# First gate block's products by quarters during the attention, and maxima over partitions by one product in other banks

## The chip, the cores and the metric

The kernel runs on one core of a Trainium2 chip. Five engines work side by side: TensorE (PE, with its weight loads as PEld), VectorE (DVE), ScalarE (ACT), GpSimd (POOL) and SyncE (SP), which issues the DMAs. Each takes its own instructions in order. The metric is the time of one execution on the device in microseconds. Products are written to PSUM, in banks of 512 fp32 columns; tiles with the same tag take turns in a fixed number of buffers.

## The reference

Three parts follow each other:

```python
x = local_plus_pooled_attention(q, k, v)        # 2 batches, 8 heads, 576 positions, width 64
x = x.transpose(0, 2, 1, 3).reshape(1152, 512)
h = silu(x @ w_gate) * (x @ w_val)              # 512 -> 1536
x = h @ w_out                                   # 1536 -> 512
P = exp(x @ moe2_w_gate - max); eight rounds of row and column normalisation; P *= N / E
out = sum over e of P[:, e:e+1] * (relu(x @ w1[e]) @ w2[e])     # 8 experts, 512 -> 1024 -> 512
```

The attention is a softmax over positions nearer than 4, plus a softmax over q, k and v averaged by fours, its result repeated four times.

## The kernel before

**Attention.** `attention()` is a generator over eight pairs of heads (`pr` 0 to 7; pairs 0 to 3 are batch 0). For each pair `scores` forms the products in three banks, the minima on DVE and 26 exponentials on ACT; POOL scales; `turn` transposes on PE and copies to SBUF (L447 to L450); `combine` forms the result, and `split` (L168, L169) writes it as two fp16 parts into `xhl`. The scores run AHEAD = 2 pairs before the rest. These banks are the tag `att` of the pool `psa`, six of them. Two more banks, the tag `y` of the pool `psg`, hold everything else: warm products (products of zeros that nothing reads: NWARM at the start, NKEEP at each of three places of pairs 0 to 3), the sums of squares of v (`x1_scale`, once for each batch), the maxima over partitions (`allmax` with `short`), and the early gate products.

**Weights.** Gate and value weights come as 64-bit floats, in twelve blocks f of 128 + 128 columns. `load_gv` loads one, `conv_gv` rebuilds fp32 from its two words (ACT and four DVE operations), `prep_gv` takes its maximum over partitions, makes a power of two of it and splits into two fp16 parts. For the first NSHORT = 5 blocks and for x, the maximum is taken by PE: a product with the identity lays the 128 values in one row, DVE reduces it, and a second product with ones brings it back to all partitions. Later blocks use POOL.

**Gate products.** `gv_step(c, f, early)` forms the products of block f with the rows of chunk c: chunk 0 has 512 columns, chunk 1 two times 320. Each product of fp32 accuracy is three fp16 products for each of four k: 24 products of 512 columns for chunk 0 (gate and value). With `early` the result goes through the two banks `y`, a Tanh on ACT and three DVE operations (L561 to L564), since the attention's table of functions stays loaded; else through larger tiles that take the attention's banks when it has ended, a Silu (L574) and one DVE operation (L575). x of pair k is what `xhl[:, :, k]` holds, so the k loop runs over pairs.

**Order.** The program gives an order by hand: after pair `pr` the loop at the end of the attention issues `gv_step(0, EARLY.index(pr), True)` where `pr` is in EARLY, then `prep_gv` and `conv_gv` by PREP and CONV. A planner then lays the instructions out on each engine by priorities and its own costs, so their order on the engine is not that of the text, except where `issue_after` (in `gate`) or `keep_in_program_order` binds it. After the attention, chunk 1's block g and chunk 0's block g + 3 alternate, with weights prepared five blocks ahead; then come the product with w_out, the routing and the experts.

Of the kernel before, what the change touches and what calls it, by code (L numbers as in the profile page):

```python
# [42 lines left out]
NABS = 5  # L43
EARLY = (4, 6, 7)
AHEAD = 2
# [6 lines left out]
HB = 4  # L52
NWARM = 5
NKEEP = 2
NQ = 3
V4B = 4
NSHORT = 5
PREP = (1, 2, 3, 5, 7)
# [6 lines left out]
def tile_kernel(ctx, tc, qT, kT, vw, vd4, wgv, wo, wg2, w1, w2, out):  # L65
# [78 lines left out]
    def absmax(o, i, axis=AX.X):  # L144
        V.tensor_reduce(o, i, axis=axis, op=ALU.max, apply_absolute_value=True)  # L145

    def allmax(mx, n, nm, short=False):

        if n > 1:
            m = tmp(1, f"gm_{nm}")  # L150
            V.tensor_reduce(m, mx, axis=AX.X, op=ALU.max)  # L151
            mx = m
        if not short:
            g = tmp(1, f"g_{nm}")
            G.partition_all_reduce(g, mx, channels=P, reduce_op=RED.max)  # L155
            return g
        ps = psg.tile([P, 512], F32, tag="y", name=f"sm_{nm}")
        r = tmp(1, f"gr_{nm}")
        T.matmul(ps[:1, :P], lhsT=mx, rhs=ident, start=True, stop=True)
        V.tensor_reduce(r[:1], ps[:1, :P], axis=AX.X, op=ALU.max)  # L160
        T.matmul(ps[:, P:P + 1], lhsT=ones[:1], rhs=r[:1], start=True, stop=True)
        return ps[:, P:P + 1]

# [43 lines left out]
    gv_src = {}  # L207

    def gate(after):
        return tc.issue_after(after.ins) if after else nullcontext()  # L210

# [126 lines left out]
    def x1_scale(b):  # L338


        ps = psg.tile([P, 512], F32, tag="y", name=f"vv{b}")[:, :P]
        n = 0
# [21 lines left out]

    exped = {}

    def attention():
# [4 lines left out]
        qd, kd, exs, ats = {}, {}, {}, {}  # L372
        summed, scaled = {}, {}

# [59 lines left out]
        def turn(pr):  # L434
            ex = exs[pr]
            nm = f"{pr}"
            pt = bank(f"t{nm}", 3)
            at = ap.tile([P, DO + 4 * SD], F32, tag="at", bufs=2, name=f"at{nm}")
            for c in range(NW):
                i, o = divmod(c * P, 512)  # L440
                T.transpose(pt[i][:, o:o + P], ex[:, c * P:(c + 1) * P], ident)
            for c in range(2):
                for t in range(NQB):
                    o = (1 - c) * P + t * 2 * HQ
                    turned[0] = T.transpose(pt[1 + c][:HS, o:o + 2 * HQ],
                                            ex[:2 * HQ, DO + t * SD + c * HS:DO + t * SD + (c + 1) * HS], ident[:2 * HQ, :2 * HQ])
            A.copy(at[:, :512], pt[0])  # L447
            A.copy(at[:, 512:DO], pt[1][:, :P])
            A.copy(at[:HS, DO:DO + 2 * SD], pt[1][:HS, P:P + 2 * SD])
            A.copy(at[:HS, DO + 2 * SD:], pt[2][:HS, :2 * SD])  # L450
            ats[pr] = at
# [38 lines left out]
        def keep_warm(pr):  # L490
            for _ in range(NKEEP if pr < NPAIR else 0):
                ps = psg.tile([P, 512], F32, tag="y", name=f"kw{pr}")
                tc.keep_in_program_order(T.matmul(ps, lhsT=warm[:, :P], rhs=warm, start=True, stop=True))
# [38 lines left out]
    gv_done = {}  # L532

    def gv_step(c, f, early):
        o, nh = CH[c]
# [16 lines left out]
        if early:  # L552

            for u in range(nu):
                pp = []
                for t in range(2):
                    ps = psg.tile([P, 512], F32, tag="y", name=f"gv{c}_{f}_{t}{u}")[:, :n]
                    products(ps, t, u)
                    pp.append(ps)
# [123 lines left out]
    for pr in attention():  # L683
# [3 lines left out]
        if pr in EARLY:  # L687
            gv_step(0, EARLY.index(pr), True)
        if pr in PREP:
            prep_gv(PREP.index(pr), x1_done[pr])  # L690
        if pr == 0:
            conv_gv(0, exped[2])
# [186 lines left out]
```

## Time and profile before

| | us |
|---|---|
| median of 3 executions | 1023.69 |
| lowest, highest | 1023.57, 1026.44 |
| profiled execution, its time | 1024.88 |
| its span in the trace | 1023.1 |
| PE busy in the span | 1006.8 |
| DVE busy | 743.1 |
| ACT busy | 444.5 |

The span is the time between the first and the last instruction of the profiled execution. Busy is time in which an engine has an instruction in work. The granted clock is a share of 2.4 GHz. Ends of matmuls are modelled, so neighbouring products overlap in their rows and the distance of starts is the better measure. In a timeline row, "x12" counts merged instructions, and the bracket at its end gives the idle time before it and what ended it.

### The profile page before, as it was taken

The numbers are of one execution on the slowest core, as the hardware profiler recorded it, in microseconds if no ns is written. First come the engines' busy times: TensorE is split into PE (matmuls) and PEld (weight loads), VectorE is DVE, ScalarE is ACT, GpSimd is POOL, SyncE is SP. The second block draws the span as 40 slices with busy tenths as digits, with TensorE's granted clock in tenths as the row PEclk, the third lists the DMA queues.
The fourth block names the chain that finished last, engine by engine and source line by source line (L and its number), as shares of the span: only waits on it lengthen the run. The fifth ranks groups of instructions, "written<-read, shape, count | busy, mean of one in ns | idle before, by whom it ended". The sixth has DMA issues, their size and how long they took to land.

```text
span 1023.1 us, 16441 instructions
## 1 busy us (share of the span) xinstructions
PE 1006.8 (98%) x6639; PEld 634.3 (62%) x6641; DVE 743.1 (73%) x1516; ACT 444.5 (43%) x926; POOL 56.9 (6%) x78
## 2 busy tenths in 40 slices
PE   8989999999999999999999999999999999999998
PEld 7765566565668657566566655756665575565644
DVE  5888788865937998797497669849757873974721
ACT  7986566665425555253235125314413521541300
POOL 4541000000001100000000000000000000000000
PEclk9989999999989999999999999999999999999999
DMA  9922143320010212121003012110301211020011
GB/s 291 277 102 97 42 165 128 121 83 1 21 63 1 84 52 73 42 81 44 5 38 122 3 42 83 43 33 9 125 1 42 83 42 42 1 83 1 1 42 52
DMA packets 12988, 67.92 MB, mean 66 GB/s; under 512 B 1584, under 2 KB 1840, under 8 KB 6512
## 3 DMA queue, kind: packets, MB, share of 16 engines
q1 hardware_dynamic: 12912, 66.87, 18.9%
q8 instruction: 52, 0.85, 0.3%
q14 instruction: 24, 0.20, 0.1%
HBM read 64.50 MB, written 2.36 MB: 65 GB/s over the span
## 4 chain that ended last, share of the span: by engine, by line
PE 77%; DVE 11%; ACT 6%; DMA 4%; issue 1%; SPq 0%; POOL 0%; ACTq 0%; DVEq 0%
PE y L176 34%; PE p L176 28%; PE gv L176 7%; PE wo L176 4%; DVE w L169 2%; DMA r<-in_w 2%; ACT ex L417 1%; DMA rawo<-in_wo 1%; DVE mxw L145 1%; DMA q<-in_qT 1%; DVE h L748 1%; PE s L402 1%; PE lgps L603 1%; DMA rawg<-in_wgv 1%; DVE cvg L203 1%
## 5 line engine op out<-in xcount | busy, mean ns | idle before, releaser
L176 PE MATMUL y<-w,hhl 128*128 128x512 f16 (+1 forms) x1752 | 396.2, 376 | 0.0
L176 PE MATMUL p<-bop,w 128*128 128x320 f16 (+1 forms) x2688 | 354.4, 286 | 1.7 <-DVE h L748 1.0
L176 PEld LDWEIGHTS <-w 128*128 128x128 f16 x2688 | 263.0, 98 | 91.8 <-issue 2.5
L176 PEld LDWEIGHTS <-hhl 128*128 128x128 f16 x1752 | 171.4, 98 | 178.2
L776 ACT ACTIVATE hhl<-h 128x640 f16<-128x640 f32 (+1 forms) x128 | 82.7, 676 | 161.6 <-DVE h L748 161.6
L176 PE MATMUL gv<-xhl,gv 128*128 128x320 f16 (+1 forms) x864 | 144.1, 328 | 1.9 <-DVE mv L357 0.8
L168 ACT ACTIVATE w<-r,s_w 128x256 f16<-128x256 f32 (+1 forms) x96 | 71.1, 783 | 117.4 <-PE y L176 86.3
L176 PEld LDWEIGHTS <-gv 128*128 128x128 f16 x864 | 84.6, 98 | 59.0 <-issue 5.6
L807 DVE SCALAR_TENSOR_TENSOR acc<-y,pe,acc 128x512 f32<-128x512 f32 (+1 forms) x64 | 47.3, 739 | 101.3 <-PE y L176 100.5
L777 DVE SCALAR_TENSOR_TENSOR hhl<-h,hhl 128x640 f16<-128x640 f32 (+1 forms) x128 | 94.1, 754 | 17.5 <-ACT hhl L776 16.6
L748 DVE SCALAR_TENSOR_TENSOR h<-p,u 128x256 f32<-128x256 f32 (+1 forms) x192 | 84.7, 453 | 15.7 <-PE p L176 9.8
L169 DVE SCALAR_TENSOR_TENSOR w<-r,s_w,w 128x256 f16<-128x256 f32 (+1 forms) x96 | 78.2, 833 | 16.8 <-ACT w L168 16.7
L176 PE MATMUL wo<-ahl,wo 128*128 128x320 f16 (+1 forms) x432 | 73.9, 333 | 0.0
L168 ACT ACTIVATE w<-cmb,s_w 128x512 f16<-128x512 f32 x64 | 43.0, 710 | 42.1 <-DVE cmb L280 40.0
L176 PEld LDWEIGHTS <-wo 128*128 128x128 f16 x432 | 43.3, 101 | 28.2
L748 DVE SCALAR_TENSOR_TENSOR u<-p,u 128x320 f32<-128x320 f32 (+1 forms) x128 | 57.4, 449 | 3.6 <-PE p L176 3.2
L765 ACT ACTIVATE s<-p 128x256 f32<-128x256 f32 (+1 forms) x64 | 25.4, 397 | 55.7 <-PE p L176 55.5
L145 DVE TENSOR_REDUCE mxw<-r 128x1 f32<-128x1024 f32 x32 | 37.4, 1213 | 16.3 <-DMA r<-in_w 16.1
L169 DVE SCALAR_TENSOR_TENSOR w<-cmb,s_w,w 128x512 f16<-128x512 f32 x64 | 46.1, 742 | 0.1
L300 ACT ACTIVATE j<-r 128x1024 f16<-128x1024 f32 x32 | 33.4, 1046 | 26.6 <-DMA r<-in_w 26.6
L155 POOL PARTITION_ALL_REDUCE g_w<-gm_w x16 | 6.3, 394 | 595.1 <-DVE gm_w L151 589.2
L748 DVE SCALAR_TENSOR_TENSOR u<-p,s 128x256 f32<-128x256 f32 (+1 forms) x64 | 28.8, 451 | 5.1 <-PE p L176 4.3
(192 smaller groups left out, 824.8 us busy)
## 6 DMA issues: line engine op xcount, KB each, us to landing
r<-in_w SPq DMA_DIRECT2D x32, 1024.0 KB, 4.8
rawg<-in_wgv SPq DMA_DIRECT2D x12, 1024.0 KB, 5.1
rawo<-in_wo SPq DMA_DIRECT2D x6, 1024.0 KB, 5.9
q<-in_qT SPq DMA_DIRECT2D x8, 576.0 KB, 6.9
vz<-in_vw SPq DMA_DIRECT2D x8, 320.0 KB, 6.7
k<-in_kT SPq DMA_DIRECT2D x8, 288.0 KB, 6.8
v<-in_vd SPq DMA_DIRECT2D x8, 288.0 KB
out<-acc SPq DMA_DIRECT2D x8, 256.0 KB, 2.0
```

What stands on the lines that cost most here:

```text
L145: V.tensor_reduce(o, i, axis=axis, op=ALU.max, apply_absolute_value=True)
L168: return (A.activation(hi, src, AF.Copy, scale=s), V.scalar_tensor_tensor(lo, src, s, hi, op0=ALU.mult, op1=ALU.subtract))
L169: V.scalar_tensor_tensor(lo, src, s, hi, op0=ALU.mult, op1=ALU.subtract))
L176: T.matmul(ps, lhsT=wf(i, k), rhs=xf(j, k), start=n == 0, stop=n == 3 * nk - 1)
L203: V.scalar_tensor_tensor(o, hi, 0xC0000000, o, op0=ALU.bitwise_and, op1=ALU.bitwise_or)
L300: A.activation(junk, t[:, 2 * j:2 * j + 2].rearrange("p a n -> p (a n)"), AF.Abs, accum_out=mx[:, 2 * i + j:2 * i + j + 1])
L402: T.matmul(ps[i][:, c * WS:(c + 1) * WS], lhsT=q[:, ws].rearrange("p s j -> p (s j)"), rhs=k[:, ws], start=False, stop=c == NW - 1)
L748: V.scalar_tensor_tensor(o, ps, HSC, u, op0=ALU.mult, op1=ALU.add)
L765: A.activation(s1, p1, AF.Copy, scale=HSC)
L776: ra = A.activation(t[:, 0], h, AF.Relu)
L777: rv = V.scalar_tensor_tensor(t[:, 1], h, 0.0, t[:, 0], op0=ALU.max, op1=ALU.subtract)
L807: V.scalar_tensor_tensor(acc[t][:, ds], ps, p[:, t:t + 1], acc[t][:, ds], op0=ALU.mult, op1=ALU.add)
```

## The change

- The first gate block (c = 0, f = 0) is no longer issued at once after pair 4. The new `gv_part(k)` issues the six products of one k, into two banks `y` that are taken at the first call and held: k = 0 and 1 after pair 1, k = 2 after pair 2, k = 3 after pair 3. `gv_step(0, 0, True)` after pair 3 then only evacuates them.
- EARLY becomes (4, 6), for blocks 1 and 2. Before, block 0 came after pair 4, block 1 after 6, block 2 after 7.
- Warm products: nine instead of five at the start; at the pairs, for pairs 0 and 1 only (KEPT = 2).
- `allmax` with `short` uses one product, its stationary operand the column of maxima repeated 128 times, its moving operand the identity, so that each partition receives all 128 values; one DVE reduction follows. The result lies in SBUF. Its bank is one of the attention's six, and so is that of the sum of squares in `x1_scale`.
- The four copies of `turn` for pair 0 run on DVE instead of ACT.

`gate` and `scaled` only change their place in the text.

```diff
--- before.py
+++ after.py
@@ -41,7 +41,7 @@
 DW = NQB * SD
 DO = NW * P
 NABS = 5
-EARLY = (4, 6, 7)
+EARLY = (4, 6)
 AHEAD = 2
 NX = 3
 WB = 6
@@ -50,11 +50,12 @@
 UB = 8
 KB = 5
 HB = 4
-NWARM = 5
+NWARM = 9
 NKEEP = 2
+KEPT = 2
+NSHORT = 5
 NQ = 3
 V4B = 4
-NSHORT = 5
 PREP = (1, 2, 3, 5, 7)
 CONV = {1: (1, 2), 3: (3,), 5: (4,), 7: (5,)}
 NCONV = 6
@@ -144,22 +145,23 @@
     def absmax(o, i, axis=AX.X):
         V.tensor_reduce(o, i, axis=axis, op=ALU.max, apply_absolute_value=True)
 
+    def gate(after):
+        return tc.issue_after(after.ins) if after else nullcontext()
+
     def allmax(mx, n, nm, short=False):
 
         if n > 1:
             m = tmp(1, f"gm_{nm}")
             V.tensor_reduce(m, mx, axis=AX.X, op=ALU.max)
             mx = m
-        if not short:
-            g = tmp(1, f"g_{nm}")
+        g = tmp(1, f"g_{nm}")
+        if short:
+            ps = psa.tile([P, 512], F32, tag="att", bufs=6, name=f"sm_{nm}")[:, :P]
+            T.matmul(ps, lhsT=mx.to_broadcast([P, P]), rhs=ident, start=True, stop=True)
+            V.tensor_reduce(g, ps, axis=AX.X, op=ALU.max)
+        else:
             G.partition_all_reduce(g, mx, channels=P, reduce_op=RED.max)
-            return g
-        ps = psg.tile([P, 512], F32, tag="y", name=f"sm_{nm}")
-        r = tmp(1, f"gr_{nm}")
-        T.matmul(ps[:1, :P], lhsT=mx, rhs=ident, start=True, stop=True)
-        V.tensor_reduce(r[:1], ps[:1, :P], axis=AX.X, op=ALU.max)
-        T.matmul(ps[:, P:P + 1], lhsT=ones[:1], rhs=r[:1], start=True, stop=True)
-        return ps[:, P:P + 1]
+        return g
 
     def split(hi, lo, src, s, pool=False):
         if pool:
@@ -205,9 +207,6 @@
         return f
 
     gv_src = {}
-
-    def gate(after):
-        return tc.issue_after(after.ins) if after else nullcontext()
 
     gv_raw = {}
 
@@ -338,7 +337,7 @@
     def x1_scale(b):
 
 
-        ps = psg.tile([P, 512], F32, tag="y", name=f"vv{b}")[:, :P]
+        ps = psa.tile([P, 512], F32, tag="att", bufs=6, name=f"vv{b}")[:, :P]
         n = 0
         with gate(turned[0]):
             for i in range(NPAIR):
@@ -362,7 +361,7 @@
             o = slice(CH[1][0], S)
             split(xhl[:, 0, :, o], xhl[:, 1, :, o], tail, x1s[1][0])
 
-    exped = {}
+    exped, scaled = {}, {}
 
     def attention():
 
@@ -370,7 +369,7 @@
             return [psa.tile([P, 512], F32, tag="att", bufs=6, name=f"{nm}_{i}") for i in range(n)]
 
         qd, kd, exs, ats = {}, {}, {}, {}
-        summed, scaled = {}, {}
+        summed = {}
 
         def pooled(pr):
             q, k = ld[pr]
@@ -444,10 +443,11 @@
                     o = (1 - c) * P + t * 2 * HQ
                     turned[0] = T.transpose(pt[1 + c][:HS, o:o + 2 * HQ],
                                             ex[:2 * HQ, DO + t * SD + c * HS:DO + t * SD + (c + 1) * HS], ident[:2 * HQ, :2 * HQ])
-            A.copy(at[:, :512], pt[0])
-            A.copy(at[:, 512:DO], pt[1][:, :P])
-            A.copy(at[:HS, DO:DO + 2 * SD], pt[1][:HS, P:P + 2 * SD])
-            A.copy(at[:HS, DO + 2 * SD:], pt[2][:HS, :2 * SD])
+            copy = A.copy if pr else V.tensor_copy
+            copy(at[:, :512], pt[0])
+            copy(at[:, 512:DO], pt[1][:, :P])
+            copy(at[:HS, DO:DO + 2 * SD], pt[1][:HS, P:P + 2 * SD])
+            copy(at[:HS, DO + 2 * SD:], pt[2][:HS, :2 * SD])
             ats[pr] = at
 
         def combine(pr):
@@ -488,7 +488,7 @@
         NP = NPAIR * B
 
         def keep_warm(pr):
-            for _ in range(NKEEP if pr < NPAIR else 0):
+            for _ in range(NKEEP if pr < KEPT else 0):
                 ps = psg.tile([P, 512], F32, tag="y", name=f"kw{pr}")
                 tc.keep_in_program_order(T.matmul(ps, lhsT=warm[:, :P], rhs=warm, start=True, stop=True))
 
@@ -531,6 +531,17 @@
     amx = {}
     gv_done = {}
 
+    held = []
+
+    def gv_part(k):
+        n = 2 * CH[0][1]
+        if not held:
+            held.extend(psg.tile([P, 512], F32, tag="y", name=f"gv0_0_{t}0")[:, :n] for t in range(2))
+        for t in range(2):
+            for i, j in ((0, 0), (0, 1), (1, 0)):
+                T.matmul(held[t], lhsT=gv_w[0][:, i, (t * KD + k) * P:(t * KD + k + 1) * P], rhs=xhl[:, j, k, :n],
+                         start=k == 0 and j == i, stop=k == KD - 1 and i > 0)
+
     def gv_step(c, f, early):
         o, nh = CH[c]
         if f == 0:
@@ -553,7 +564,9 @@
 
             for u in range(nu):
                 pp = []
-                for t in range(2):
+                for t in range(0 if f else 2):
+                    pp.append(held[t])
+                for t in range(2 if f else 0):
                     ps = psg.tile([P, 512], F32, tag="y", name=f"gv{c}_{f}_{t}{u}")[:, :n]
                     products(ps, t, u)
                     pp.append(ps)
@@ -685,9 +698,14 @@
             load_gv(0)
             continue
         if pr in EARLY:
-            gv_step(0, EARLY.index(pr), True)
+            gv_step(0, 1 + EARLY.index(pr), True)
         if pr in PREP:
             prep_gv(PREP.index(pr), x1_done[pr])
+        if 0 < pr < KD:
+            for k in range(0 if pr == 1 else pr, pr + 1):
+                gv_part(k)
+            if pr == KD - 1:
+                gv_step(0, 0, True)
         if pr == 0:
             conv_gv(0, exped[2])
             load_gv(1)
```

## Rows read from the trace of the kernel before

**Rows 1.** Busy time, share of the span and instructions of each engine, whole execution.
```profile
PE 1006.8 (98%) x6639; PEld 634.3 (62%) x6641; DVE 743.1 (73%) x1516; ACT 444.5 (43%) x926; POOL 56.9 (6%) x78
```

**Rows 2.** Windows: length, busy us (instructions) of each engine, granted clock, DMA.
```profile
0.00:98.10 98.10, 89.39 (x859) 66.54 (x862) 75.97 (x173) 77.01 (x305) 38.81 (x46) 0.95 0.61 191
98.10:108.90 10.80, 10.80 (x53) 4.73 (x52) 8.24 (x13) 5.87 (x10) 0.00 (x0) 1.00 0.18 77
108.90:230.90 122.00, 120.90 (x772) 75.43 (x772) 96.53 (x180) 79.41 (x140) 4.38 (x8) 1.00 0.31 113
```

**Rows 3.** Windows of 10 us, same columns.
```profile
60.00:70.00 10.00, 7.23 (x91) 5.63 (x91) 8.08 (x15) 8.01 (x36) 6.69 (x8) 1.00 0.40 139
70.00:80.00 10.00, 9.22 (x53) 5.19 (x53) 8.51 (x25) 6.58 (x29) 3.37 (x4) 0.50 0.00 1
80.00:90.00 10.00, 10.00 (x104) 5.85 (x103) 8.46 (x18) 7.77 (x16) 2.17 (x3) 0.99 0.43 140
```

**Rows 4.** Timeline of PE: start, us, line, operation, count, idle before.
```profile
1.17 2.31 PE L90 MATMUL pw<-warm 128*128 128x512 bf16 x5 [1.17 <-DVE dist L93]
5.32 0.72 PE L399 MATMUL s<-maskb,identb 128*128 128x320 bf16 x2 [1.83 <-DVE identb L107]
5.82 4.51 PE L402 MATMUL s<-k,q 128*128 128x64 f32 x20
...
20.99 2.44 PE L402 MATMUL s<-k,q 128*128 128x64 f32 x20 [0.87 <-ACT k L380]
...
54.81 0.38 PE L493 MATMUL kw<-warm 128*128 128x512 bf16 x1
...
64.61 0.38 PE L159 MATMUL sm_v<-ident,mxv 128*1 128x128 f32 x2 [0.48 <-DVE mxv L354]
...
76.29 4.65 PE L176 MATMUL gv<-xhl,gv 128*128 128x512 f16 x12 [0.78 <-DVE mv L357]
...
82.92 2.75 PE L176 MATMUL gv<-xhl,gv 128*128 128x512 f16 x12
...
98.10 10.53 PE L176 MATMUL gv<-xhl,gv 128*128 128x512 f16 x48
...
199.47 31.42 PE L176 MATMUL gv<-xhl,gv 128*128 128x320 f16 x216 [0.46 <-ACT act L574]
```

**Rows 5.** Timeline of DVE in the attention.
```profile
22.36 0.49 DVE L409 TENSOR_REDUCE stm<-s 128x5 f32<-128x320 f32 x1
...
51.27 1.28 DVE L169 SCALAR_TENSOR_TENSOR gv<-cvg,s_gv,gv 128x1024 f16<-128x1024 f32 x1
...
62.74 1.21 DVE L169 SCALAR_TENSOR_TENSOR xhl<-x,s_x,xhl 128x512 f16<-128x512 f32 x1
...
70.63 0.27 DVE L160 TENSOR_REDUCE gr_v<-sm_v 1x1 f32<-1x128 f32 x1
...
76.09 0.15 DVE L357 TENSOR_SCALAR mv<-sm_v 128x1 uint32<-128x1 uint32 x1
```

**Rows 6.** Warm products of the pairs: ns minimum/median/maximum, first and last start.
```profile
L493 PE MATMUL kw<-warm x22: 376/379/390, 19.5 to 54.8; 128*128 128x512 bf16 x22
```

**Rows 7.** Timeline of DVE at the end of the attention.
```profile
98.90 0.81 DVE L481 TENSOR_TENSOR x<-o,avd 128x288 f32<-128x288 f32 x2
...
102.71 0.48 DVE L562 TENSOR_SCALAR act<-act,iv 128x512 f32<-128x512 f32 x1
...
105.44 0.74 DVE L564 SCALAR_TENSOR_TENSOR act<-gv,iv,act 128x512 f32<-128x512 f32 x1
```

**Rows 8.** Timeline of ACT in the attention.
```profile
19.75 0.61 ACT L447 COPY at<-t 128x512 f32<-128x512 f32 x1
...
79.59 0.51 ACT L168 ACTIVATE xhl<-tail,s_x 128x256 f16<-128x256 f32 x1 [2.73 <-DVE s_x L140]
```

**Rows 9.** Chain that ended last, pieces between 160 and 200 us.
```profile
166.92 0.71 ACT act L574
...
175.65 7.48 DMA rawo<-in_wo
```

## The prediction

> **What bounds the kernel now.** I read the page first. TensorE (PE) is busy 1006.8 of 1023.1 us [rows 1], so PE work sets the end, unless work is put where PE would have stood still or has run slowly. The windows come next, cut at the end of the attention [rows 2]. From 98.1 to 230.9 us, where the gate and value products run, PE is idle 1.1 us in all (10.80 - 10.80, 122.00 - 120.90). In the first 98.1 us it is idle 8.7 us, and its mean granted clock is 0.95. So a microsecond of products moved from behind 98.1 to a free place before it is worth about a microsecond.
>
> The finer windows show where the free places are [rows 3]: 60 to 70 us has 2.8 us of PE idle time. In 70 to 80 the granted clock is 0.50, the lower level, 1.2 GHz: the 9.22 us of work there would fit in some 4.6 us at 2.4 GHz. Before that fall PE was partly idle and had almost only fp32 products; it rose again while the first 16-bit gate products ran. The PE timeline prices this [rows 4]: the first half of the first gate block takes 4.65 us for twelve products, the second 2.75 us for the same twelve. In the attention DVE and ACT are nearly as full as PE (8.08 and 8.01 of 10 us in 60 to 70), so its length hangs on all three.
>
> **The block that moves.** Four blocks of 24 products with 512 columns lie between 76.29 and 108.6 us: three early ones and the main one for f = 3. The last 48 of these products run from 98.10 on, back to back, 10.53 / 48 = 0.219 us each [rows 4]. After the change block 0 comes behind pairs 1 to 3 and the other early blocks one slot earlier each, so of the 48 only 24 are left behind the attention. This takes 24 x 0.219 = 5.3 us off a stretch where PE is the bound.
>
> What does block 0 cost where it goes? Its weights are ready at 51.27 + 1.28 = 52.55 us and the last quarter of its input at 62.74 + 1.21 = 63.95 [rows 5], so it can be issued between about 52.6 and 65 us: 18 products first, 6 after. That is 5.3 us of PE time. Twelve of the 24 warm products go at the same time (KEPT is 2, so those of pairs 2 and 3), 0.22 us each if back to back as the gate products, 0.38 by their own rows [rows 4, 6]: -2.6 to -4.6 us. Net +0.7 to +2.7 us of PE work, against 2.8 us of idle time in 60 to 70 [rows 3]. I take the cost as nothing, covered by that idle time; uncovered it is +2.7 us.
>
> **Evacuation.** Block 2's three DVE operations come at 102.71 (0.48), 103.71 (0.68 by the pattern of the other two blocks) and 105.44 (0.74) [rows 7], behind the attention. They move into it: about 1.9 us on DVE, and two passes over the block on ACT, about as long. DVE has 1.5 us free in each of 70 to 80 and 80 to 90 [rows 3]. Hidden or not, bounds 0 and +1.9; I take +0.5.
>
> **The copies for pair 0.** Four copies leave ACT, where they start at 19.75 with one of 0.61 us [rows 8], in a part where ACT works through exponentials without a gap, and go to DVE. By the nearest row, a reduction of 320 columns from the same kind of bank in 0.49 us [rows 5], their 1216 columns cost about 1.9 us of DVE. DVE has room there; ACT can scale the next k 0.5 us sooner. Bounds -0.9 to +1.0; I take -0.4.
>
> **The maxima.** Before, a maximum is a product, a DVE reduction, a second product and a read by the next DVE operation. After, it is one product (with a 128-column instead of a 1-column weight) and one reduction. Each of seven maxima loses one pair of products, about 0.3 us of PE, and one round trip. One round trip was dear: the second batch's maximum is reduced at 70.63 and only read at 76.09 [rows 5], the first gate product waited 0.78 us for that read, and ACT stood still 2.73 us until the scale came [rows 4, 8]. The two rows do not add: ACT's idle time here is not all on the path. Bounds 0 to -2.7; I take -1.0.
>
> The banks are the new wait. Nine results (two sums of squares, seven maxima) now take turns with the scores in the attention's six banks, where each pair takes eight. The reduction of such a result sits in DVE's order; until it is done the sixth tile after it, a score or transpose group of a later pair, can't start, and behind that PE instruction everything queues. Before, such results sat in the other two banks and hurt little when late (the second batch's maximum was multiplied at 64.61 and reduced at 70.63 [rows 4, 5]). Nothing shows the cost in the new place: below 0 (the banks turn over faster), above several microseconds. The nearest row is the read at 76.09 that held the gate product for 0.78 us; I take +0.8, once.
>
> **The warm products.** Five take 2.31 us from 1.17 on, 0.43 us apart. Nine end near 5.2 us, and the first score product waits until 5.32 for the identity [rows 4]: they lie in the 1.83 us that PE waits anyway. The first scores show the lower clock, the third pair no longer (20 products in 4.51 us, at 20.99 in 2.44 [rows 4]). If the nine bring the rise forward, PE gains some 4 us in a part where ACT's chain of exponentials sets the pace, so I count 0, bounds 0 and -1.5.
>
> **The clock in 70 to 80.** With block 0 issued between 52 and 65 us in place of fp32 work and idle time, the fall is likelier to stay away than not. If it stays away, the twelve products that took 4.65 us take 2.75: -1.9 us on the path [rows 4]. I take -1.2, between 0 and -1.9; all of the lost 4.6 us is the lower end.
>
> **Hand-over.** Before, block 2 covers the time in which the attention's banks come free for the larger tiles of the main blocks (the last pair's sums on DVE run from 98.90, 0.81 us [rows 7]). After, that cover is gone or thinner: 0 to +1.6; I take +0.8.
>
> **Behind it.** Weights must keep up with a PE that is early. The chain from 166.92 to 199.47 runs over ACT, DVE and a load of 7.48 us [rows 9] and ends in PE, which had been idle only 0.46 us there [rows 4]. The chain starts from a PE result at 166.92, so it moves with PE in the main, but its DVE work does not get shorter. Bounds 0 and +5.3; I take +0.6.
>
> **Sum.** -5.3 + 0 + 0.5 - 0.4 - 1.0 + 0.8 + 0 - 1.2 + 0.8 + 0.6 = -5.2 us. The profiled execution took 1024.88 us (span 1023.1), 1.2 above the median 1023.69, which is what a change of this size is to be set against. 1023.7 - 5.2 = 1018.5 us.
>
> **Rivals.**
> - *Clock and attention close up (0.18).* The clock stays at 2.4 GHz from 5 us on, the 4.6 us of 70 to 80 and much of ACT's 2.73 us come back: -5.3 - 4.6 + 0.5 = about 1014. For it: ACT and DVE both wait on PE in 70 to 82. Against: DVE is 85% busy there.
> - *The clock falls where warm products go (0.06).* Pairs 2 and 3 lose twelve warm products, and before 52.6 us no quarter can stand in for them. A fall like that at 70, ten microseconds at 1.2 GHz, costs 4.6 us, and the gain of 1.2 in 70 to 80 is lost: 1023.7 - 5.2 + 1.2 + 4.6 = 1024.3, no change. For it: the fall at 70 came with no warm product since 54.81 [rows 4]. Against: the pairs' products leave PE hardly any idle time before 58 us. The Trainium skill, "TensorE: Matmul & The Clock Gate", Part 1, states this as a rule: the lower clock is the default, and activity releases it; here the trace agrees with it for 76 to 80 us, where dense gate products came before the rise, and not for the time from 5.3 us to the second pair, where PE was busy with fp32 scores almost without a gap and stayed at the lower clock.
> - *The block only changes place (0.16).* The attention is itself bound, 30 to 58 us by PE, then by DVE; block 0 pushes it back by its net 2.7 us and block 2's evacuation by 1.9, or the weights chain gives the 5.3 us back near 199 us. 1021 to 1024: no change. For it: DVE and ACT are above 80% in 60 to 70 us. Against: PE's idle time there.
> - *The bank ring stalls (0.10).* Slower. The place is a score group of pair 4 to 7 held by a maximum whose reduction is late in DVE's order. One of 5 us eats the gain; two of 7 us, somewhat longer than the 6.0 from 64.61 to 70.63, give 1023.7 - 5.2 + 14 - 3 = 1029.5, with 3 us of them in idle time. It decides from 5.2 + 3.1 = 8.3 us of lost attention time on. Against: the order on DVE is laid out anew with the banks known.
>
> **How the numbers follow.** The main case has 0.50, with its own range 1015 to 1020.6. A change under 0.3%, 3.1 us, can't be told from none. Faster: 0.50 + 0.18 = 0.68; same: 0.06 + 0.16 = 0.22; slower: 0.10. The range 1010.5 to 1024.5 takes in the bounds of the clock terms below and the unchanged case above, and leaves out the slow rival and a little below.
>
> **What would show it.** In the new profile: 24 gate products of 512 columns between 52 and 66 us; no more than about 24 between the last attention product and the first 320-column product; that first product near 103 instead of 108.9; a granted clock near 1.00 in 60 to 90 us; nothing over 1 us of PE waiting for a maximum's reduction. The prediction is wrong if the attention ends more than 3 us later than 98 us, or if PE is idle several microseconds between 110 and 231 us. A new fall of the clock behind 231 us, where the order of instructions is laid out anew as well, would move the time by some 3 us without any of these steps being wrong.

## The result, and the profile after

| | before | after |
|---|---|---|
| median of 4 executions, us | 1024.07 | 1033.66 |
| lowest, highest | 1023.57, 1026.44 | 1032.04, 1036.05 |
| profiled execution: span | 1023.1 | 1030.1 |
| first gate product behind the attention, start | 98.10 | 111.39 |
| first gate product of 320 columns, start | 108.88 | 119.15 |
| first product with w_out, start | 230.73 | 242.23 |
| first product of the experts' stage, start | 312.32 | 320.52 |

The ratio is 1.0100, 95% interval 1.0078 to 1.0122: slower by 1%, where 0.5% faster was forecast, and outside the range. By the starts in the table the attention takes 13.3 us more, the gate stage 1.8 less, the product with w_out 3.3 less and the rest 1.2 less, in all +7.0 us of span. At the first gate product of 320 columns both kernels have done the same work, the attention and 96 products of 512 columns; the new one comes there 10.3 us later.

The page's busy line of the kernel after answers to [rows 1]: PE is busy 6.6 us less, in a longer span.

```profile
PE 1000.2 (97%) x6618; PEld 631.8 (61%) x6619; DVE 745.7 (72%) x1520; ACT 444.2 (43%) x922; POOL 55.3 (5%) x78
```

The windows of the stages, cut at the start of the last attention products, at the first gate product behind them, at the first of 320 columns and at the first with w_out (columns as in [rows 2]), and then windows of 10 us, to be held against [rows 3]:

```profile
0.00:106.95 106.95, 88.28 (x847) 66.80 (x848) 79.50 (x181) 78.21 (x306) 37.07 (x46) 0.87 0.57 179
106.95:111.39 4.44, 1.33 (x23) 1.15 (x21) 2.52 (x6) 1.44 (x4) 0.00 (x0) 0.50 0.24 98
111.39:119.15 7.76, 7.76 (x24) 2.96 (x25) 6.49 (x16) 4.46 (x6) 0.35 (x1) 0.66 0.17 33
119.15:242.23 123.08, 120.48 (x770) 75.10 (x769) 93.73 (x167) 77.46 (x137) 4.23 (x7) 1.00 0.30 110
...
10.00:20.00 10.00, 4.99 (x32) 4.37 (x33) 4.44 (x13) 7.28 (x44) 6.34 (x9) 0.71 1.05 284
40.00:50.00 10.00, 9.13 (x71) 7.62 (x75) 9.21 (x20) 7.76 (x32) 4.09 (x5) 0.58 0.57 188
60.00:70.00 10.00, 5.39 (x96) 4.80 (x95) 6.50 (x19) 7.93 (x32) 2.63 (x3) 0.94 0.41 140
70.00:80.00 10.00, 10.00 (x48) 8.82 (x47) 8.12 (x26) 6.48 (x28) 1.58 (x3) 0.54 0.00 0
```

In the attention PE has about as much work as before (88.28 against 89.39 us) and twice the idle time (18.7 against 8.7), at a mean granted clock of 0.87 instead of 0.95. (Both means leave out the start: before, the column reads 1.00 in the first 20 us, while twenty scores take 4.51 us there and 2.44 at 20.99 [rows 4].) Three stretches hold time at the lower level, 1.2 GHz: 10 to 20, 40 to 50 and 70 to 80 us; before, from 20 us on, there was one, the 0.50 of [rows 3].

The PE timeline of the kernel after shows what comes ahead of each of them:

```profile
1.17 3.50 PE L91 MATMUL pw<-warm 128*128 128x512 bf16 x9 [1.17 <-DVE dist L94]
...
5.81 2.44 PE L401 MATMUL s<-k,q 128*128 128x64 f32 x20
...
16.97 1.33 PE L440 MATMUL t<-ident,ex 128*128 128x128 f32 x5 [4.79 <-POOL ex L427]
...
37.16 0.49 PE L160 MATMUL sm_gv<-ident,mxg 128*128 128x128 f32 x2 [1.33 <-ACT rawg L225]
37.48 0.60 PE L440 MATMUL t<-ident,ex 128*128 128x128 f32 x4
39.24 0.33 PE L440 MATMUL t<-ident,ex 128*128 128x128 f32 x1 [1.16 <-ACT ex L416]
...
40.29 0.44 PE L444 MATMUL t<-ident,ex 96*72 96x96 f32 x3 [0.47 <-ACT ex L420]
...
42.05 4.53 PE L401 MATMUL s<-k,q 128*128 128x64 f32 x20
...
50.45 3.41 PE L542 MATMUL gv<-xhl,gv 128*128 128x512 f16 x12
...
69.51 0.77 PE L160 MATMUL sm_v<-ident,mxv 128*128 128x128 f32 x2 [4.61 <-DVE mxv L353]
70.07 0.64 PE L160 MATMUL sm_gv<-ident,mxg 128*128 128x128 f32 x2
70.50 1.27 PE L440 MATMUL t<-ident,ex 128*128 128x128 f32 x5
...
77.11 1.06 PE L542 MATMUL gv<-xhl,gv 128*128 128x512 f16 x2
...
111.39 11.20 PE L178 MATMUL gv<-xhl,gv 128*128 128x512 f16 x48 [3.11 <-DVE g_gv L161]
123.14 3.15 PE L178 MATMUL gv<-xhl,gv 128*128 128x320 f16 x22 [0.56 <-DVE act L588]
```

(A merged row names only its first shape: of the 48 products at 111.39, 24 have 512 columns and 24 have 320.) At 37.16 and 69.51 PE stands at a maximum over partitions whose operand is not ready, and the transposes of the next pair (`t`) stand behind it, here those of pairs 2 and 4. The maxima of weight blocks (`sm_gv`) at 37.16 and 70.07, and two more at 53.70 and 94.11, each stand right ahead of a pair's transposes. Before, they had places of their own; its PE timeline for the same pairs:

```profile
35.94 0.77 PE L441 MATMUL t<-ident,ex 128*128 128x128 f32 x5
...
39.49 0.38 PE L159 MATMUL sm_gv<-ident,mxg 128*1 128x128 f32 x2
...
53.50 0.76 PE L441 MATMUL t<-ident,ex 128*128 128x128 f32 x5
```

Pair 2's transposes come 1.5 us later than before, and behind them the scores of pair 4 take 4.53 us, at half rate. The maximum is not the last thing that pair 2 waits for. Its own exponentials were scaled by 29.8 us, and yet its fifth transpose waits 1.16 us, and its last three 0.47, for exponentials of pair 3. That is the turn of the banks: a pair takes eight tiles (three for transposes, three for scores, two for results) out of six buffers, so before the change its three transpose tiles take over the buffers of the last transpose tile of the pair before and of the first two score tiles just written. With one maximum in between they take over those of all three score tiles, which ACT must have read first; and ACT ends these exponentials at 40.2 us, before at 36.6. Pair 4's transposes come at 70.50 instead of 53.50, and behind them the granted clock is 0.54. At 111.39 the main gate products wait 3.11 us for the reduction of a weight maximum, which frees the bank that they take: its product comes at 105.90, and DVE reduces it at 111.04, behind sums and splits of the last pair. The nine warm products do what was hoped of them at 5.81 (2.44 us in place of 4.51 [rows 4]), and then PE stands still for 4.79 us, because POOL, which waited 12.6 us for the load of v, can't scale pair 0 sooner, and the clock is lost again (0.71 in 10 to 20 us).

DVE of the same kernel between 62 and 71 us, where PE waits 4.61 us:

```profile
62.63 1.56 DVE L171 SCALAR_TENSOR_TENSOR gv<-cvg,s_gv,gv 128x1024 f16<-128x1024 f32 x1 [0.67 <-ACT gv L170]
64.11 0.59 DVE L410 TENSOR_REDUCE stm<-s 96x3 f32<-96x432 f32 x1
67.40 0.19 DVE L424 TENSOR_REDUCE rs<-sts 128x16 f32<-128x32 f32 x1 [2.69 <-ACT ex L420]
...
69.07 0.29 DVE L353 TENSOR_TENSOR mxv<-mxv,mxv 128x1 f32<-128x1 f32 x1
```

The value that PE waits for needs two short DVE operations. They stand behind a sum of pair 5 that waits 2.69 us for ACT's exponentials. So pair 4's transposes, whose exponentials were long done, wait on PE for those of pair 5.

### The profile page after: what moved, and what is told of

The parts are those of the page before. It is cut to its first block, busy times and chain, and to the rows that moved or that the text cites. A ratio compares the mean times of both kernels' runs of the same rounds, so it can differ in the third digit from the quotient of the medians.

```text
span 1030.1 us, 16399 instructions
## 1 busy us (share of the span) xinstructions
PE 1000.2 (97%) x6618; PEld 631.8 (61%) x6619; DVE 745.7 (72%) x1520; ACT 444.2 (43%) x922; POOL 55.3 (5%) x78
## 4 chain that ended last, share of the span: by engine, by line
PE 79%; DVE 11%; ACT 5%; DMA 2%; issue 2%; SPq 0%; POOL 0%; ACTq 0%; DVEq 0%; POOLq 0%
PE y L178 36%; PE p L178 31%; PE wo L178 4%; PE gv L178 4%; DMA rawo<-in_wo 1%; DVE cvg L205 1%; DVE cvg L206 1%; DMA v<-in_vd 1%; PE s L401 1%; ACT ex L416 1%; DVE cvg L200 1%; DVE act L588 1%; DVE w L171 1%; ACT rawg L225 1%; PE lgps L616 1%
## 5 line engine op out<-in xcount | busy, mean ns | idle before, releaser
L178 PE MATMUL gv<-xhl,gv 128*128 128x320 f16 (+1 forms) x840 | 139.4, 328 | 5.7 <-DVE g_gv L161 3.1
L178 PEld LDWEIGHTS <-gv 128*128 128x128 f16 x840 | 82.5, 99 | 61.0 <-issue 7.5
L178 PE MATMUL wo<-ahl,wo 128*128 128x320 f16 (+1 forms) x432 | 71.5, 326 | 0.0
L171 DVE SCALAR_TENSOR_TENSOR ahl<-act,sc,ahl 128x512 f16<-128x512 f32 (+1 forms) x24 | 19.6, 818 | 17.6 <-ACT ahl L170 17.6
```

The costliest lines, as they stand in the source:

```text
L171: V.scalar_tensor_tensor(lo, src, s, hi, op0=ALU.mult, op1=ALU.subtract))
L178: T.matmul(ps, lhsT=wf(i, k), rhs=xf(j, k), start=n == 0, stop=n == 3 * nk - 1)
```

## The experiments

Times are medians in us, ratios are to the kernel before on the same chip, with 95% intervals.

**Which part of the change costs it.** e1 puts only the new `allmax` and the new bank of `x1_scale` into the kernel before (both hunks as in the diff).

> The kernel before, with one part of the change alone: maxima by one product, and they and the sums of squares in the attention's six banks. Bank theory (the results in the attention's banks hold up the scores): the attention ends 5 us or more later, 1029 or slower. Quarter theory (the products of block 0 between the scores hold them up) and clock theory (missing warm products bring half-clock stretches): no part of either is in it, 1021 to 1025, the round trip saved being worth at most 2.7 us.

1035.70, ratio 1.0114 (1.0089 to 1.0140): the whole loss. e2 has only the nine warm products.

```diff
-NWARM = 5
+NWARM = 9
```

> The kernel before with nine warm products at the start and nothing else. All three theories: 1022 to 1025 (first scores at the full clock, but the third pair waits for a load of v through POOL, as in the changed kernel). A gain of 2 us or more would mean that the start sets the attention's length after all; a loss of 3 us or more would mean that the clock, raised early and lost again behind 12 us, is a cost of its own.

1024.81, 1.0018 (0.9987 to 1.0049): no change that can be told. e3 is the change without the quarters (EARLY as before); e4 is the change with NWARM = 5.

> The changed kernel without its quarters: block 0 whole behind pair 4 and blocks 1 and 2 behind 6 and 7 as before; maxima in the attention's banks, nine warm products at the start, none at pairs 2 and 3, copies of pair 0 on DVE. Quarter theory: the loss is gone, 1021 to 1025. Bank theory: most of it stays, 1029 to 1034. Clock theory: it stays or grows, as neither warm products nor quarters stand at pairs 2 and 3: 1031 to 1038.

> The changed kernel with five warm products at the start instead of nine. Bank and quarter theory: 1031 to 1036 as the changed kernel, since pairs 0 and 1 wait for a load anyway. Clock theory: within 3 us of it, the half-clock stretches at 40 to 50, 70 to 80 and 105 to 115 us being made by what comes later.

1034.58, 1.0103 (1.0066 to 1.0140), and 1036.69, 1.0129 (1.0100 to 1.0158). Neither the quarters nor the warm products at the start explain the loss.

**One product, or its bank?** e5 keeps the one product and leaves it in the old banks, the sums of squares too (shown against the line of e1):

```diff
-            ps = psa.tile([P, 512], F32, tag="att", bufs=6, name=f"sm_{nm}")[:, :P]
+            ps = psg.tile([P, 512], F32, tag="y", name=f"sm_{nm}")[:, :P]
```

> The kernel before with maxima by one product and one reduction, in the two banks they had before; the sums of squares stay there too. Bank theory: no loss, 1019 to 1025, with a gain of up to 2.7 us from the shorter round trip. Product theory (the 128-column product or the order it brings is itself the cost, whatever the bank): 1030 or slower.

1021.83, 0.9971 (0.9948 to 0.9994): a gain of 3 us. e6 is the kernel before, with its two products, and only the weights' maxima in the attention's banks:

```diff
-        ps = psg.tile([P, 512], F32, tag="y", name=f"sm_{nm}")
+        ps = (psa.tile([P, 512], F32, tag="att", bufs=6, name=f"sm_{nm}") if nm[0] == "g" else
+              psg.tile([P, 512], F32, tag="y", name=f"sm_{nm}"))
```

> The kernel before, maxima by two products as before, but those of the five weight blocks lie in the attention's six banks; x's stay in the two others. Bank theory in the form that the weights' maxima, which take a bank in turn and so tie the rebuilding of a weight block to the next pair's transposes, are the cost: 1030 to 1036. In the form that x's sums of squares and maxima are the cost: 1022 to 1026. Product theory: 1022 to 1026.

1034.32, 1.0103 (1.0066 to 1.0140). The bank of five small results alone makes the kernel before 1% slower. Its PE timeline:

```profile
35.77 1.25 PE L494 MATMUL kw<-warm 128*128 128x512 bf16 x5
38.96 0.38 PE L160 MATMUL sm_gv<-ident,mxg 128*1 128x128 f32 x2 [1.94 <-ACT rawg L227]
39.27 0.77 PE L442 MATMUL t<-ident,ex 128*128 128x128 f32 x5
...
41.44 2.24 PE L403 MATMUL s<-k,q 128*128 128x64 f32 x10
...
63.85 0.38 PE L160 MATMUL sm_gv<-ident,mxg 128*1 128x128 f32 x2 [2.57 <-DVE mxv L353]
...
111.89 0.40 PE L162 MATMUL sm_gv<-gr_gv,ones 1*128 1x1 f32 x2 [3.10 <-DVE gr_gv L161]
```

It resembles the kernel after: a maximum ahead of pair 2's transposes, a wait for the weights' conversion on ACT, scores at half the rate (2.24 us for ten), and a wait of 3.10 us at the hand-over. Banks of one tag are given out in the order of the text, and there the weight block stands ahead of the next pair's transposes; in the pool of its own it could be laid behind them. The first product of 320 columns comes at 119.5 us, 10.6 later than before. About half of that is the attention: it ends 10.6 us later (108.8 against 98.2) and holds 24 more products of 512 columns, 24 x 0.219 = 5.3 us. The other half is the hand-over: 3.4 us until the first gate product, and 7.3 us for 24 products.

The Trainium skill, "Perfetto Trace Analysis", section "Matmuls", would have independent products rotate through different banks, so that the evacuation of one lies beside the next. Here the five maxima take turns in six banks instead of two, and the kernel is 1.0% slower.

e7 is the counterpart: one product, x's sums and maxima in the attention's banks, the weights' in the old ones.

> The kernel before with maxima by one product, the weights' in the two other banks, x's two sums of squares and two maxima in the attention's banks. Bank theory with the weights as the cost: 1020 to 1026. With x's results as the cost (the product that waited 4.6 us for the sum in the changed kernel): 1028 or slower. Product theory: 1030 or slower.

1022.15, 0.9982 (0.9965 to 1.0000): in the kernel before it is the weights' banks that cost, not x's.

**Is it the order alone?** e9 leaves the banks of before and binds the transposes behind the weight maximum's product:

```diff
-        T.matmul(ps[:1, :P], lhsT=mx, rhs=ident, start=True, stop=True)
+        mm = T.matmul(ps[:1, :P], lhsT=mx, rhs=ident, start=True, stop=True)
+        if nm[0] == "g":
+            ahead[0] = mm
...
+            with gate(ahead[0]):
+                for c in range(NW):
```

> The kernel before with its banks and its two products, and one order added on PE: the transposes of a pair are issued behind the product of the last weight maximum that stands ahead of them in the text, as they are with that product in the attention's banks. Order theory (the bank only does harm by putting a weight block's maximum ahead of the next pair's transposes): the loss is there without any change of banks, 1030 to 1036. Occupancy theory (a bank of the six held until DVE has read it is itself the cost): no loss, 1021 to 1027.

1026.54, 1.0027 (1.0009 to 1.0044). By its expectation this speaks against the order as the whole cause. The last attention products end at 106.78 instead of 98.17, 8.6 us later; at the first product of 320 columns (115.6) 6.7 us of it are left, against 10.6 in e6, and in the median of the whole kernel 2.5. What came back behind that product was not followed. Gate products start at 106.71, with no wait at the hand-over. And the clock behaves differently behind the same wait:

```profile
40.62 0.38 PE L161 MATMUL sm_gv<-ident,mxg 128*1 128x128 f32 x2 [1.88 <-ACT rawg L230]
40.93 0.77 PE L446 MATMUL t<-ident,ex 128*128 128x128 f32 x5
...
42.39 1.22 PE L406 MATMUL s<-k,q 128*128 128x64 f32 x10
```

Here PE waits 1.88 us ahead of pair 2's transposes, and 1.90 ahead of pair 3's, and the granted clock is 1.00 from 40 to 60 us; in e6 it falls behind a wait of 1.94 (0.52 in 40 to 50). So order is part of the cause and not shown to be all of it, and such a wait alone does not decide whether the clock falls.

e10 gives the weights' maxima a bank of their own and the attention five; e8 takes the maxima with POOL (NSHORT = 0).

> The changed kernel with five banks for the attention and x's results, and one bank of its own for the weights' maxima. Order theory: the transposes no longer stand behind the maxima, the loss is mostly gone, 1015 to 1026, unless five banks are too few for scores and transposes of three banks each, then 1030 or slower. Occupancy theory: five banks are as bad as six with visitors, 1032 or slower.

> The changed kernel with the weights' maxima on POOL as the later blocks have them, so that they need no bank; x's results stay in the attention's banks, quarters and warm products as changed. Bank theory with the weights as the cost: the loss is gone, 1015 to 1026, and the 5.3 us of the moved block should begin to show. With x's results as the cost: 1028 to 1034. Quarter theory: 1030 or slower.

e10: 1034.41, 1.0110 (1.0081 to 1.0139). The loss stays, although the turn of the banks no longer puts a weight maximum ahead of the transposes. Its PE timeline:

```profile
36.27 0.60 PE L441 MATMUL t<-ident,ex 128*128 128x128 f32 x4
37.07 0.49 PE L161 MATMUL sm_gv<-ident,mxg 128*128 128x128 f32 x2 [0.20 <-ACT rawg L226]
39.16 0.33 PE L441 MATMUL t<-ident,ex 128*128 128x128 f32 x1 [1.60 <-ACT ex L417]
...
40.21 0.44 PE L445 MATMUL t<-ident,ex 96*72 96x96 f32 x3 [0.48 <-ACT ex L421]
```

The maximum waits 0.20 us here, and the transposes still wait for pair 3's exponentials, until the same time as in the kernel after (40.21 against 40.29); the clock falls alike (0.57 in 40 to 50, 0.55 in 70 to 80). With five buffers for eight tiles the three transpose tiles take over those of the three score tiles in every pair, as they do with six and a maximum. So the wait that ends last here in the kernel after is that for a bank, not that for the operand of the maximum at 37.16. How much of the 1% it is worth is not shown, as e10 also has x's results in these banks and the new start. e8: 1045.60, 1.0218 (1.0156 to 1.0281), the attention ends at 123.7 us: POOL, which scales the exponentials too, is a worse place here.

**What is left without the weights in those banks.** e12 is the kernel after with the weights' maxima in the old banks; as block 0 holds both of them, the preparation of the two blocks that fall at pairs 2 and 3 is moved behind its evacuation (PREP 1, 3, 4, 5, 7). e16 is e12 with the old start: five warm products, pair 0's copies on ACT.

> The changed kernel with the weights' maxima in the two old banks: block 0's before the quarters take these, those of blocks 1 and 2 after block 0 has been evacuated, one slot later in the text (PREP 1, 3, 4, 5, 7). x's results stay in the attention's banks; quarters, nine warm products and none at pairs 2 and 3 as changed. If the weights' maxima in the attention's banks are the only cost of the change: 1012 to 1020. If the quarters between the scores, or the missing warm products, cost as much again: 1028 or slower. Between them, 1020 to 1028, a part is theirs.

> The changed kernel with the weights' maxima in the old banks (1030.87), with five warm products at the start and the copies of pair 0 on ACT again; quarters and x's results in the attention's banks stay. If the start costs: 1018 to 1026. If the quarters or x's results do: 1028 to 1033.

1030.87, 1.0073 (1.0057 to 1.0090), and 1022.79, 0.9992 (0.9971 to 1.0014). Taken out of the kernel after, the weights' banks give back 0.27% (1.0100 to 1.0073), inside the two intervals, though put into the kernel before they cost 1.03%. The new start then costs 0.8% (e12 against e16). The old start with the whole rest only draws level with before.

**Without quarters.** e11 is e5 with one more edit, the blocks issued whole but earlier; e13 is e11 without the warm products of pairs 2 and 3; e14 is e11 with x's sums and maxima in the attention's banks; e15 is e14 with the new start and without those warm products.

```diff
-EARLY = (4, 6, 7)
+EARLY = (3, 4, 6)
```

> The kernel before with maxima by one product in the old banks (1021.8 in its own run) and the early blocks one slot earlier each, block 0 whole behind pair 3, block 1 behind 4, block 2 behind 6; no quarters. If the term of 5.3 us for a block moved from behind the attention is right: 1015 to 1019. If the attention is itself full, so that the block only changes place: 1020 to 1025. If evacuations and products in pair 3 hold up the scores: 1026 or slower.

> The kernel of 1016.05 us (one product in the old banks, early blocks behind pairs 3, 4 and 6) without the warm products of pairs 2 and 3. Clock theory: half-clock stretches between 40 and 65 us, 1020 or slower. If the work of the pairs keeps the clock up as long as nothing waits: 1013 to 1019.

> The kernel of 1016.05 us with x's two sums of squares and two maxima moved to the attention's banks, the weights' maxima left in the old ones. If x's results in the attention's banks cost something once the block stands behind pair 3 (the product of the second batch's maximum waited 4.6 us in front of the transposes of pair 4 in the changed kernel): 1020 or slower. If only the weights' maxima do: 1013 to 1019.

> The kernel of run e14 with the rest of the change but the quarters: nine warm products at the start, none at pairs 2 and 3, copies of pair 0 on DVE. If the quarters are what costs in the changed kernel with the old banks (1030.87): 1013 to 1021. If the start (early rise and fall of the clock, copies that DVE waits for) is: 1024 or slower.

| | median | ratio | interval |
|---|---|---|---|
| e11 | 1016.05 | 0.9912 | 0.9883 to 0.9942 |
| e13 | 1016.62 | 0.9933 | 0.9908 to 0.9958 |
| e14 | 1022.13 | 0.9985 | 0.9971 to 0.9999 |
| e15 | 1029.95 | 1.0068 | 1.0043 to 1.0093 |

e11 beats both kernels. Its windows in the attention:

```profile
20.00:30.00 10.00, 9.78 (x127) 8.27 (x126) 5.73 (x11) 7.25 (x34) 6.86 (x9) 1.00 1.00 358
40.00:50.00 10.00, 9.67 (x111) 7.96 (x111) 9.35 (x22) 10.00 (x42) 3.59 (x6) 1.00 0.89 287
60.00:70.00 10.00, 9.46 (x98) 6.37 (x97) 8.53 (x27) 7.87 (x34) 4.77 (x5) 1.00 0.37 117
70.00:80.00 10.00, 10.00 (x111) 7.81 (x110) 10.00 (x17) 8.08 (x34) 5.13 (x5) 1.00 0.18 56
```

The clock stays at 2.4 GHz, PE idles 1.1 us of these 40, and the last attention product ends at 95.5 us, as in e5 (95.6; 98.17 before), although block 0 lies between them. Against e5 the early blocks give 0.59%, 6 us (2 to 10 by the two intervals). e13 is 0.2% above e11, inside the intervals, so no cost of leaving out the warm products of pairs 2 and 3 is shown; but its trace, of the slowest of its four executions, has the clock at 0.50 in 50 to 60 us, where e11 has 1.00. By e14, x's results in the attention's banks cost 0.7% here, while in e7, against e5, they cost nothing that can be told (0.11%). e16 equals e14 within the intervals: with quarters or with whole blocks after pair 3, the time is the same.

**The start taken apart.** e17 is e14 with nine warm products alone, e18 is e14 with pair 0's copies on DVE alone.

> The kernel of e14 (blocks after pairs 3, 4 and 6, x's sums and maxima in the attention's banks, one product each; 1022.13 us) with nine warm products at the start and nothing else. e15, which has the nine warm products, fewer warm products at the pairs and pair 0's copies on DVE, took 1029.95. If the nine warm products alone bring the loss (first scores at the higher clock, PE then idle about 5 us until POOL has scaled pair 0, clock back at the lower level), this run takes 1028 to 1031 us, and the granted clock between 15 and 30 us is below 0.8. If the copies on DVE bring it, this run takes 1021 to 1024. If it takes both together, both runs stay near 1022 to 1024.

> The kernel of e14 (1022.13 us) with pair 0's four copies on DVE in place of ACT and nothing else. If the copies bring the loss of the new start (DVE stands at the copies, waiting for PE's transposes, and the minima and conversions behind them start late), this run takes 1028 to 1031 us. If the warm products bring it, 1021 to 1024, and a copy waits no more than 2 us.

e17: 1028.31, 1.0018 (0.9990 to 1.0045). e18: 1027.03, 1.0026 (1.0002 to 1.0050). Above e14 that is 0.33% and 0.41%, together 0.74%, where e15, which also lacks the warm products of pairs 2 and 3, lies 0.83% above it: about half each, with intervals too wide to rank them. Neither alone is the whole cost of the start. The profiled execution of e17 shows the pattern of the kernel after:

```profile
5.81 2.44 PE L401 MATMUL s<-k,q 128*128 128x64 f32 x20
...
16.48 1.33 PE L440 MATMUL t<-ident,ex 128*128 128x128 f32 x5 [4.22 <-POOL ex L427]
...
19.94 4.37 PE L401 MATMUL s<-k,q 128*128 128x64 f32 x20
```

What the early rise gives (2.1 us at 5.81) is lost at 19.94, where these scores took 2.44 us before [rows 4]. Its ten executions go from 1023.1 us, at a mean granted clock of 0.988, to 1034.2, at 0.979; the profiled one, at 0.978, took 1033.05, so it shows the costly case, not the middle one. e18 has a wait of 1.7 us of a copy on DVE for PE's transposes, and the clock at 0.54 in 40 to 50 us.

## Why the prediction was wrong

**The step that failed** is "The banks are the new wait", with its "+0.8, once". By e6 it is 1.03%, 10.5 us. By e1 against e5, which differ in the banks alone, x's included, it is 1.43%, 14.7 us; the one product gives 3 of it back in e1. The place was wrong with the size. The prediction, and its rival of the bank ring, looked for a score group of pair 4 to 7 held by a maximum *reduced* late on DVE. In the attention, PE waits for two other things. One is the *operand* of a maximum, since the turn of the banks puts this product ahead of the transposes: the whole rebuilding of a weight block (1.33 us after, 1.94 in e6), or the sums of squares of v, whose maximum stands in the same line (4.61 us; in e6 a weight maximum waits 2.57 us, put down to the same operation). The other is the score tiles of the next pair, which the transposes must follow once an extra tile has moved the turn on (1.16 and 0.47 us after, 1.60 and 0.48 in e10). Behind these waits the clock falls in the kernel after and in e6, though not in e9 behind 1.88 us; where it falls, the work up to the next dense gate products goes at half the rate. Only at the hand-over does PE wait for a late reduction, as the paragraph has it, 3.11 us. The rival had the direction, by a wait that is seen only there; its time, 1029.5, is 4 us short.

**The block that moves: -5.3.** Right as a price, and lost here. e11 against e5 gives 6 us. As forecast, 24 products of 512 columns are left between the attention and the first of 320 columns; but this comes at 119.15 us, not near 103. In the kernel after, the attention is so long that it would hold three early blocks in any order: in e3, without quarters, 72 of the 512-column products lie ahead of the attention's end as well (so they do in e1 and e6), and the quarters bring 0.9 us (1034.58 to 1033.66, inside the intervals). Of the gate stage's 5.3 us, 1.8 are seen: the 24 products behind the hand-over take 7.8 us at a granted clock of 0.66 instead of 24 x 0.219 = 5.3, and PE's idle time behind them is 2.6 us, 1.5 more than the whole stage had before. These 4.0 us are a little more than the 3.5 that are missing.

**Block 0's place: 0.** It holds: e11 puts 24 products there and the attention ends no later than in e5, and e16 equals e14. In the kernel after, 18 of them came between 50.5 and 60 us as forecast, the last six only at 77 to 80.

**The copies: -0.4, and the warm products: 0.** Both were mis-sized, some 3 to 4 us each by e18 and e17 against e14. In the kernel before, nine warm products can't be told from none by the interval of e2, but its ten executions fall into two groups, five from 1021.5 to 1023.4 us (granted clock 0.987 to 0.990) and four from 1029.1 to 1031.4 (0.977 and 0.978), as those of e17 do; so they may cost something there too. I counted PE's early clock as free and did not ask what PE would do when it was done sooner: it waits for POOL.

**The maxima: -1.0.** Right in sign, the size by e5 is -3.0 us (-5.3 to -0.6), at the far end of the bounds.

**The clock in 70 to 80: -1.2.** Right where block 0 stands behind pair 3 and nothing else disturbs (e11: 1.00 from 20 to 90 us), not here (0.54).

**Hand-over: +0.8.** Mis-sized: of the 4.44 us from 106.95 to 111.39, the work is 1.33 us at half rate, so 3.8 us are lost, and 2.5 more in the 24 products behind it. It is not all the banks' doing: in e11 PE waits 1.8 us there at a maximum for a weight block's conversion, and the 24 products behind it take 6.3 us (granted clock 0.81). **Weights chain: +0.6.** PE's idle time behind the hand-over grew by 1.5 us, but its waits there are for DVE's last operation on finished blocks (L588, 2.6 us), which is not shown to be the weights. **Evacuation: +0.5.** Not told apart.

**Behind 231 us.** The forecast allowed for a new fall of the clock there; the opposite came. The fall that before has at 290 to 295 us (granted 0.50) is not in this execution (1.00), which gives most of the 3.3 us of the stage. It is not shown to be the change's: over the traces of the twenty kernels this stage takes 78.3, about 80, 81.6 or 83.3 us, the shortest in e18, which has little of the change, the longest in e4, which has all but four warm products.

The losses do not add up. Weights' banks alone cost 10.5 us in the kernel before, x's results in the banks 0.7% (e14 against e11) and the new start 0.8% (e12 against e16, e15 against e14), and all of them together 1%: each makes PE wait and the clock fall in the same part of the attention. That one covers the other there is argued from the windows, not shown; e12, where the weights' banks give back only 0.27%, fits it. By the traces e6's loss is about half attention and half hand-over. Open is how the attention's part splits into order, turn of the banks and clock, since e9's order alone gave a longer attention and only 0.27% in total, and e10 the same loss without the weights' order. Each edit also lets the planner lay out the instructions anew, and what such a new layout is worth by itself was not tried.

## What to carry to other kernels

Before a small result is put into the banks of another stage, read the order in which those banks are given out: the result then stands in that stage's line with everything it waits for, not only with its own 0.3 us, and it moves every later tile on by one bank. Move work into a gap one edit at a time and look at the granted clock of the stretches behind it; here the plain move was worth 0.6% on top of the one product (e11 against e5; 0.9% together), and x's results in the banks and the new start each took some of that back. Raising the clock early was worth nothing here, where PE then had to wait for POOL.

## What the runs showed of the hardware that was not expected

- Twenty fp32 score products take 4.51 us behind five warm products and 2.44 behind nine. After that PE stands idle for 4.79 us, and the next five transposes take 1.33 us, against 0.71 at 28.77 in the same trace. The Trainium skill, "TensorE: Matmul & The Clock Gate", Part 1, has it that the throttled state is the default and activity releases it. These rows agree in both directions; the kernel before does not quite, as PE is busy there with fp32 scores from 5.3 to 17.7 us and twenty of them take 4.51 us.
- One program's time goes with its mean granted clock from execution to execution, if not strictly: the nineteen of the kernel before that stand beside e17 go from 1022.0 us at 0.993 to 1031.3 at 0.983. An effect of 0.3% needs many executions here.
- A maximum over partitions by one product with a 128 times repeated stationary column and one reduction costs 0.49 and 0.28 us by its rows and saves a round trip, together worth 3 us over seven maxima (e5, 0.6 to 5.3).
